# Delta-rule attention and an expert router on one core: chunks of 32 tokens of all four sequences in place of 64 tokens of two, and two expert tiles beside the last chunks

## The chip, the core and the metric

The kernel runs on one core of a Trainium2 chip. A core has TensorE (PE, matrix products; PEld are its weight loads), VectorE (DVE), ScalarE (ACT), GpSimd (POOL), and queues that start DMA transfers (SP is the engine whose queue starts most of them here). Each engine works through its own list of instructions in the order in which the program gives them; engines wait for each other by semaphores. Matrix products read SBUF and write PSUM, eight banks of 512 fp32 columns on 128 partitions. The metric is device microseconds (us) of one launch. The profile is one more execution, so its span differs a little from the times.

## The reference

Four sequences of 768 tokens, eight heads of 48 columns. Each head of each sequence has a state of 48x48, which every token changes (the delta rule). The outputs, with the heads side by side, are 3072 rows of 384, and go through a router to one of eight experts each.

```python
k_n = k / (np.linalg.norm(k, axis=-1, keepdims=True) + 1e-06)
for t in range(S):                                   # 768 tokens
    y[:, :, t] = einsum('bhd,bhde->bhe', q[:, :, t], state)
    v_old = einsum('bhde,bhd->bhe', state, kt)
    state = state + bt * einsum('bhd,bhe->bhde', kt, vt - v_old)
# x: (3072, 384)
logits = xn @ en.T / tau                             # rows and expert embeddings normed
expert_idx = argmax(logits, axis=1);  gate_w = softmax(logits)[expert_idx]
for e in range(8):
    h = np.maximum(x[mask] @ w1[e], 0.0)             # w1[e]: 384 x 1024
    out[mask] = gate_w[mask, None] * (h @ w2[e])     # w2[e]: 1024 x 384
```

All products are in fp32.

## The kernel before

The tokens are handled in chunks. Inside a chunk, the rule becomes products with a triangular matrix and its inverse, which is built by doubling blocks: from inverses of 2x2 blocks to 4, 8, 16 and 32. A *unit* is one chunk of 64 tokens of two sequences: 128 rows (partitions), 16 matrices of 64x64 (two sequences, eight heads). There are 12 chunks times two pairs of sequences, 24 units; the two pairs alternate, so a unit needs the state that the unit two before it left. All small products go through one helper line, `mm` (L286), which is why most groups of the profile have that line; the tile names tell them apart.

```python
C = 64
PERIOD = 20
HALF = (slice(0, C), slice(C, 2 * C))
def mm(out_, lhsT, rhs, start=True):
    nc.tensor.matmul(out_, lhsT=lhsT, rhs=rhs, start=start, stop=True, skip_group_check=True)
# ... cut: loads, norms of k (prep1..3; the power is GpSimd's), transposes of K and Q by TensorE
def flip(src):                       # 128x128 transposes by TensorE, two 64x64 blocks each
    p = bank(jc)
    for j in range(NP):
        nc.tensor.transpose(p[:, j]..., src[:, j]..., ident)
    return p
def t_flip(U, eng):
    p = flip(U["W"])
    U["T"] = work("T", 3)
    eng(U["T"], p)
def product(lhsT, rhs):              # input half a, output half b: all four 64x64 tiles
    p = pair([NP, C])
    for j in range(NP):
        for a in range(2):
            for b in range(2):
                mm(p[HALF[b], a, j], lhsT[HALF[a], j, b], rhs[HALF[a], j, b])
    return p.rearrange("p a j c -> p j a c")
def level(U, s, by):
    p = product(U["A"][by], U["T"])
    U["P"] = PP[s][U["n"] % 2]
    nc.vector.copy_predicated(U["P"], below[s].broadcast_to(jc), p)
def grow(U):
    p = product(U["P"], U["W"])
    U["W"] = work("W", 5)
    act_copy(U["W"], p)
def apply(lhsT, rhs):                # input half = output half
    p = bank([128, H, D])
    for h in range(H):
        for i in range(2):
            mm(p[HALF[i], h], lhsT[HALF[i], h // 2, h % 2], rhs[HALF[i], h])
    return p
def solve1(U): ...  # Z1 = first half of apply(W, R)
def solve2(U): ...  # R += second half of apply(A, Z1)
def solve3(U): ...  # Z = apply(W, R): the step from 32 to 64 tokens
# ... cut: gram (16 products of 128 columns), q_state and k_state (16 each), state (16), outputs (apply),
#          x_transposes, logits (two halves), route1..3: choice of the expert, ranks, gate
def route4(c, xc, ssx, lz):          # once for two chunks
    for g in range(G):               # G = 4: running counts of each expert
        nc.vector.tensor_tensor(rk[:, 0, g], rk[:, 0, g], run, op=ALU.add)
        nc.vector.tensor_tensor(run, run, rk[:, 1, g], op=ALU.add)
    # ... cut: slot_i, each token's place in its expert's list
    for g in range(G):
        nc.gpsimd.indirect_dma_start(out=idmap[:, :],
            out_offset=bass.IndirectOffsetOnAxis(ap=slot_i[:, g:g + 1], axis=0),
            in_=K["tokid"][:, c - 1 + g // NU, g % NU:g % NU + 1], in_offset=None)
PLAN = [(-60, load_kq), (-46, prep1), (-42, prep2), (-36, prep3), ..., (5, gram), (9, a_flip),
        (13, lambda U: level(U, 2, 1)), (16, grow), (19, lambda U: t_flip(U, nc.vector.tensor_copy)), ...]
steps = [(U["n"] * PERIOD + at, i, U["n"]) for U in UNITS for i, (at, _) in enumerate(PLAN) if i or U["n"]]
for _, i, n in sorted(steps): ...    # this order is the order of each engine's list
```

Then come the experts. A tile is 128 rows of one expert. Eight lists of unknown length need at most 24 + 7 = 31 tiles, and 31 are always run; each fetches its list of rows, its expert's weights (two transfers of 1536 KB) and its rows.

```python
NT = N // T + E - 1                  # 31
ahead = [fetch(0), fetch(1)]
xT = transposed(ahead[0][-1])
for i in range(NT):
    now = ahead.pop(0)
    if i + 2 < NT:
        ahead.append(fetch(i + 2))
    nxT = transposed(ahead[0][-1]) if ahead else None
    experts(xT, *now)                # 24 products of 128 columns, Relu, 8 products of 384 columns
    xT = nxT
```

Of the kernel before, what the change touches and what calls it, by code (L numbers as in the profile page):

```python
# [13 lines left out]
SP = mybir.EngineType.SP  # L14

C = 64
T = 128
LEVELS = (2, 4, 8, 16)


@with_exitstack
def kernel(
# [35 lines left out]


# [3 lines left out]
    NU = B // 2  # L63
# [3 lines left out]
    NMAP = E * N + NT * T  # L67
# [4 lines left out]
    run = cpool.tile([128, E], F32, name="run")  # L72
    K = {}
    x_dram = tc.dram_tile([N + 1, Dm + 1], F32, name="x_dram")
    idmap = tc.dram_tile([NMAP, 1], I32, name="idmap")

    def bank(shape):
        return ps.tile(shape, F32, name="bank", tag="bank", bufs=2)

    def pair(shape):  # L80

        t = ps.tile([128, 2, 512], F32, name="pair", tag="pair", bufs=3)
        n = 1
        for d in shape:
            n *= d
        t = t[:, :, 0:n]
        if len(shape) == 2:
            return t.rearrange("p r (a b) -> p r a b", a=shape[0])
        return t.rearrange("p r (a b c) -> p r a b c", a=shape[0], b=shape[1])
# [7 lines left out]
    hc = [128, H, C]  # L97
    jc = [128, NP, 2, C]


    def padded(name, bufs):

        ts = []
        for i in range(bufs):
            t = ac.tile(hc, F32, name=f"{name}{i}")
            nc.gpsimd.memset(t[:, :, D:C], 0.0)
            ts.append(t)
        return ts

    def load(U, dst, src):  # L110

        t0 = U["c"] * C
        for i in range(2):
            nc.sync.dma_start(out=dst[i * C:(i + 1) * C],
                              in_=src[2 * U["u"] + i, :, t0:t0 + C, :].rearrange("h p d -> p h d"))

    def load_kq(U):
        U["k"] = io.tile([128, H, D], F32, name="k_in", tag="k_in", bufs=4)
        load(U, U["k"], k)
        U["Q"] = QQ[U["n"] % len(QQ)]  # L120
        load(U, U["Q"][:, :, 0:D], q)
# [5 lines left out]
    UNITS = [dict(n=n, c=n // NU, u=n % NU) for n in range(NC * NU)]  # L127
    QQ = padded("QQ", 4)
    load_kq(UNITS[0])
    bt = ac.tile([NU * H, NC, 2, C], F32, name="bt")  # L130
    for u in range(NU):
        for i in range(2):
            nc.scalar.dma_start(out=bt[u * H:(u + 1) * H, :, i],
                                in_=beta[2 * u + i].rearrange("h (c t) -> h c t", t=C))
    emb = ac.tile([E, Dm], F32, name="emb")
    nc.scalar.dma_start(out=emb, in_=moe_expert_emb)
    rtau = ac.tile([128, 1], F32, name="rtau")
    nc.scalar.dma_start(out=rtau, in_=moe_tau.broadcast_to([128, 1]))
# [4 lines left out]
    half = cpool.tile([128, NU, H], F32, name="half")  # L143
    nc.vector.memset(half, 0.5)
    KK = padded("KK", 6)


    prow = ac.tile([128, C], I32, name="prow")
    nc.gpsimd.iota(prow, pattern=[[0, C]], base=0, channel_multiplier=1)
    xor_i = ac.tile([128, C], I32, name="xor_i")  # L150
    nc.gpsimd.iota(xor_i, pattern=[[1, C]], base=0, channel_multiplier=0)
    trow = ac.tile([128, C], I32, name="trow")
    nc.vector.tensor_single_scalar(trow, prow, C - 1, op=ALU.bitwise_and)
    col_f = ac.tile([128, C], F32, name="col_f")
    nc.vector.tensor_copy(col_f, xor_i)
    nc.vector.tensor_tensor(xor_i, xor_i, trow, op=ALU.bitwise_xor)
    xor_f = ac.tile([128, C], F32, name="xor_f")
    nc.vector.tensor_copy(xor_f, xor_i)
    trow_f = ac.tile([128, C], F32, name="trow_f")
# [3 lines left out]
    id64 = ac.tile([128, 1, C], F32, name="id64")  # L163
    nc.vector.tensor_single_scalar(id64[:, 0, :], xor_f, 0.0, op=ALU.is_equal)
    upper = ac.tile([128, 1, C], F32, name="upper")
    nc.vector.tensor_tensor(upper[:, 0, :], col_f, trow_f, op=ALU.is_gt)
    lower = ac.tile([128, 1, C], F32, name="lower")
    nc.vector.tensor_tensor(lower[:, 0, :], col_f, trow_f, op=ALU.is_lt)

    def filled(name, bufs, value):  # L170

        ts = []
        for i in range(bufs):
            t = ac.tile(jc, F32, name=f"{name}{i}")
            nc.scalar.activation(t.rearrange("p j r c -> p (j r) c"), id64.broadcast_to(hc), ACT.Copy, scale=value)
            ts.append(t)
        return ts

    def mask(name, tri, lo, hi):
        m = ac.tile([128, 1, 1, C], F32, name=name)  # L180
        nc.vector.scalar_tensor_tensor(out=m[:, 0], in0=xor_f.unsqueeze(1), scalar=float(lo), in1=tri,
                                       op0=ALU.is_ge, op1=ALU.mult)
        nc.vector.scalar_tensor_tensor(out=m[:, 0], in0=xor_f.unsqueeze(1), scalar=float(hi), in1=m[:, 0],
# [3 lines left out]
    W2 = filled("W2_", 2, -1.0)  # L187
    T2 = filled("T2_", 2, -1.0)
    up2 = mask("up2", upper, 1, 2)
    below = {s: mask(f"below{s}", lower, s, 2 * s) for s in (1,) + LEVELS}  # L190


    psB = bank([128, NC, NU * H])
    for c in range(NC):
        nc.tensor.transpose(psB[:, c], bt[:, c].rearrange("p i t -> p (i t)"), ident[0:NU * H, 0:NU * H])
    betaT = ac.tile([128, NC, NU * H], F32, name="betaT")
    nc.vector.tensor_copy(betaT, psB)
    sqb = ac.tile([128, NC, NU * H], F32, name="sqb")
    nc.scalar.activation(sqb, betaT, ACT.Sqrt)
    quot = ac.tile([128, NC, NU * H], F32, name="quot")  # L200
    nc.vector.tensor_scalar_max(sqb, sqb, 1e-30)
    nc.vector.reciprocal(quot, sqb)
# [487 lines left out]
```

## Time and profile before

| what | value |
|---|---|
| median of 2 runs | 902.03 us (900.04 to 904.02) |
| span of the profile | 888.4 us, mean TensorE clock 0.919 |
| busy PE / DVE / ACT / POOL | 738.4 / 292.1 / 245.9 / 224.1 us |
| last copy of logits (end of attention but for the routing) | 497.9 us |
| first matmul of an expert's hidden layer | 541.7 us |
| last result of an expert (y) | 878.6 us |

The costliest groups of the page:

```profile
L639 PE MATMUL acc<-xTm,w 128*128 128x128 f32 x1488 | 172.3, 276 | 0.0
L644 PE MATMUL acc<-w,hT 128*128 128x384 f32 x496 | 165.1, 486 | 0.0
L286 PE MATMUL pair<-W,P 64*64 64x64 f32 x3072 | 75.9, 232 | 42.1 <-DVE P L376 35.0
L286 PE MATMUL bank<-Z,G 64*64 64x48 f32 x1536 | 60.4, 231 | 5.2 <-issue 4.1
L286 PE MATMUL bank<-R,W 64*64 64x48 f32 x1536 | 59.5, 230 | 0.9 <-issue 0.6
L346 PE MATMUL bank<-ident,W 128*128 128x128 f32 x288 | 49.2, 295 | 11.1 <-ACT KT L362 10.1
```

A line names the engine, the operation, the output tile, an arrow and the inputs, then the shape and the number of instructions; after the bar stand busy time in us and the mean ns of one, after the second bar the idle time before it and who ended it. An fp32 product is two instructions: 24 units x 4 steps x 16 products of `grow` are 1536, and the row with W and P has 3072. Matmuls are pipelined, so the mean of one (232 ns) is not the distance between two.

### The profile page before, as it was taken

Reading aid. Unit: us, or ns where it says so; the run is one execution under the profiler, and the core shown is the slowest. Engines: PE = TensorE matmul, PEld = TensorE weight load, DVE = VectorE, ACT = ScalarE, POOL = GpSimd, SP = SyncE. Lnnn points to the kernel's source line nnn. Section 1 sums busy time; section 2 is a strip of 40 time slices with the busy share of each in tenths; the row PEclk is TensorE's granted clock in tenths of the full one; section 3 lists DMA queues with packets and bytes.
Section 4 is the critical chain, followed back from the end, with each engine's and each line's share of the span. In section 5 each row is a group of like instructions: output and inputs, shape, how many; then the busy total and the mean of one; then the engine's idle time right before and its main releaser. Section 6 shows DMA issues by size and latency. Waiting matters only on the chain. (4 is left out here: it accounts for less than half of the span.)

```text
span 888.4 us, 33205 instructions
## 1 busy us (share of the span) xinstructions
PE 738.4 (83%) x15148; PEld 632.6 (71%) x15148; DVE 292.1 (33%) x692; ACT 245.9 (28%) x468; POOL 224.1 (25%) x240
## 2 busy tenths in 40 slices
PE   1589998598599859897988306999999999999995
PEld 1578887587588758787877205888888877777774
DVE  5356555356265625544553400000000000000000
ACT  4245453254344324533433100111111111111110
POOL 4543341333243233414111111121111111111110
PEclk9799997799989769978989657999999999999998
DMA  4332122122221211120010149999999999999940
GB/s 85 77 66 49 31 53 52 20 52 40 45 49 35 62 29 35 27 48 3 5 39 4 36 152 374 322 321 326 329 321 329 314 341 327 320 315 320 318 163 1
DMA packets 134190, 129.64 MB, mean 146 GB/s; under 512 B 84538, under 2 KB 119521, under 8 KB 134050
## 3 DMA queue, kind: packets, MB, share of 16 engines
q1 hardware_dynamic: 128738, 116.55, 43.0%
q0 software_dynamic: 4736, 10.85, 3.6%
q8 instruction: 119, 1.95, 0.9%
q10 hardware_dynamic: 576, 0.11, 0.1%
q14 instruction: 21, 0.17, 0.1%
HBM read 117.91 MB, written 10.95 MB: 145 GB/s over the span
## 5 line engine op out<-in xcount | busy, mean ns | idle before, releaser
L639 PE MATMUL acc<-xTm,w 128*128 128x128 f32 x1488 | 172.3, 276 | 0.0
L639 PEld LDWEIGHTS acc<-xTm,w 128*128 128x128 f32 x1488 | 169.9, 193 | 0.3
L644 PE MATMUL acc<-w,hT 128*128 128x384 f32 x496 | 165.1, 486 | 0.0
L644 PEld LDWEIGHTS acc<-w,hT 128*128 128x128 f32 x496 | 91.9, 190 | 57.5
L641 ACT ACTIVATE hT<-acc 128x512 f32<-128x512 f32 x62 | 37.0, 597 | 337.5 <-PE acc L639 291.3
L646 DVE TENSOR_SCALAR y<-acc,xg 128x384 f32<-128x384 f32 x31 | 19.1, 617 | 304.2 <-PE acc L644 304.2
L286 PE MATMUL pair<-W,P 64*64 64x64 f32 x3072 | 75.9, 232 | 42.1 <-DVE P L376 35.0
L286 PEld LDWEIGHTS pair<-W,P 64*64 64x64 f32 x3072 | 66.0, 144 | 45.0 <-DVE P L376 36.2
L362 ACT ACTIVATE W<-pair 128x512 f32<-128x512 f32 x96 | 57.5, 599 | 119.8 <-PE pair L286 118.6
L376 DVE COPY_PREDICATED P<-below,pair 128x512 f32<-128x512 int32 x96 | 70.5, 735 | 49.4 <-PE pair L286 49.4
L647 POOL DMA_INDIRECT out_dram<-y,ids x31 | 31.5, 1016 | 164.1 <-DVE y L646 161.4
L301 POOL TENSOR_TENSOR rn<-rn,half 128x8 f32<-128x8 f32 x24 | 39.5, 1646 | 110.4 <-DVE rn L300 109.6
L286 PE MATMUL bank<-Z,G 64*64 64x48 f32 x1536 | 60.4, 231 | 5.2 <-issue 4.1
L620 POOL DMA_INDIRECT xg<-x_dram,ids x31 | 30.0, 968 | 136.1 <-DMA ids<-idmap 73.7
L286 PE MATMUL bank<-R,W 64*64 64x48 f32 x1536 | 59.5, 230 | 0.9 <-issue 0.6
L286 PEld LDWEIGHTS bank<-Z,G 64*64 64x64 f32 x1536 | 55.4, 147 | 6.8 <-issue 4.7
L346 PE MATMUL bank<-ident,W 128*128 128x128 f32 x288 | 49.2, 295 | 11.1 <-ACT KT L362 10.1
L538 POOL DMA_INDIRECT idmap<-tokid,slot_i x24 | 23.8, 991 | 132.8 <-DMA idmap<-tokid,slot_i 65.6
L286 PEld LDWEIGHTS bank<-R,W 64*64 64x64 f32 x1536 | 55.8, 148 | 1.5 <-issue 0.6
L629 PE MATMUL acc<-ident,xg 128*128 128x128 f32 x93 | 16.0, 283 | 38.8 <-DMA xg<-x_dram,ids 38.8
L629 PEld LDWEIGHTS acc<-ident,xg 128*128 128x128 f32 x93 | 12.3, 146 | 48.5 <-issue 35.7
L286 PE MATMUL pair<-T,AJ 64*64 64x64 f32 x1536 | 43.3, 244 | 3.5 <-DVE T L354 2.8
(161 smaller groups left out, 895.5 us busy)
## 6 DMA issues: line engine op xcount, KB each, us to landing
w<-in_moe_w_dram SPq DMA_DIRECT2D x62, 1536.0 KB
x_dram<-xc SPq DMA_DIRECT2D x24, 192.5 KB
k_in<-in_k_dram SPq DMA_DIRECT2D x48, 96.0 KB
QQ<-in_q_dram SPq DMA_DIRECT2D x48, 96.0 KB
v_in<-in_v_dram SPq DMA_DIRECT2D x48, 96.0 KB
ids<-idmap SPq DMA_DIRECT2D x31, 0.5 KB
xg<-x_dram,ids POOLq DMA_INDIRECT x31, 6.6
out_dram<-y,ids POOLq DMA_INDIRECT x31, 7.1
```

What stands on the lines that cost most here:

```text
L286: nc.tensor.matmul(out_, lhsT=lhsT, rhs=rhs, start=start, stop=True, skip_group_check=True)
L301: nc.gpsimd.tensor_tensor(out=U["rn"], in0=U["rn"], in1=half[:, 0], op=ALU.pow)
L346: nc.tensor.transpose(p[:, j].rearrange("p r c -> p (r c)"), src[:, j].rearrange("p r c -> p (r c)"), ident)
L362: nc.scalar.activation(out_, in_, ACT.Copy)
L376: nc.vector.copy_predicated(U["P"], below[s].broadcast_to(jc), p)
L538: nc.gpsimd.indirect_dma_start(out=idmap[:, :], out_offset=bass.IndirectOffsetOnAxis(ap=slot_i[:, g:g + 1], axis=0), in_=K["tokid"][:, c - ...
L620: nc.gpsimd.indirect_dma_start(out=x, out_offset=None, in_=x_dram[:, :], in_offset=bass.IndirectOffsetOnAxis(ap=ids[:, 0:1], axis=0))
L629: nc.tensor.transpose(psX[:, j, :], x[:, j * 128:(j + 1) * 128], ident)
L639: nc.tensor.matmul(psH[:, i, :], lhsT=w1[:, j, (f + i) * 128:(f + i + 1) * 128], rhs=xT[:, j, :], start=(j == 0), stop=(j == KC - 1))
L641: nc.scalar.activation(hT[:, f:f + 4, :], psH, ACT.Relu)
L644: nc.tensor.matmul(psO, lhsT=hT[:, f, :], rhs=w2[:, f, :], start=(f == 0), stop=(f == NF - 1))
L647: nc.gpsimd.indirect_dma_start(out=out[:, :], out_offset=bass.IndirectOffsetOnAxis(ap=ids[:, 0:1], axis=0), in_=y, in_offset=None, bounds_ ...
```

## The change

A unit becomes one chunk of 32 tokens of all four sequences: again 128 rows and 24 units, but 32 matrices of 32x32, two of which share a 64x64 block. Now each unit needs the state that the unit just before it left. The doubling ends at 32 tokens, so one solve step is enough. Transposes inside the doubling are made by VectorE in 32x32 blocks, in place of TensorE's 128x128. The fixed period is replaced by a table of places (KEYS and BASE) that orders all parts, and a part can be split in stages. PSUM banks are handed out by hand. List entries of one group are declared free of one another; the last group is smaller (two units). Early tiles: after 16 chunks the first two tiles of expert 0's list are taken, and worked on beside the last units, with expert 0's weights loaded during attention. The rest of the experts' tiles run under two branches, so that tiles beyond the count are skipped in steps.

```diff
-C = 64
+C = 32
+PC = 2 * C
+GROUP = 4
+AHEAD_AT = 16
+AHEAD = 2
...
+    CORNERS = ((0, 0), (1, 1), (0, 1), (1, 0))
...
+    def transposed_blocks(U, src):
+        U["T"] = wk.tile([128, H, C], F32, name="T", tag=f"T{U['n'] % 3}", bufs=1)
+        nc.vector.transpose(U["T"].rearrange("p h c -> p (h c)"), src.rearrange("p h c -> p (h c)"))
...
+    def apply(lhsT, rhs, at=by_number, rat=by_number, to=None, times=1):
+        n = rhs.shape[2]
+        p = bank([128, times, H, n])
+        for h in range(H):
+            for i in range(2):
+                (half_, l), (_, r) = at(i, h), rat(i, h)
+                own = HALF[half_]
+                mm(p[own, :, (to or rat)(i, h)[1]], lhsT(i, h) if callable(lhsT) else lhsT[own, l],
+                   rhs[own, r].unsqueeze(1).broadcast_to([PC, times, n]))
+        return p if times > 1 else p[:, 0]
+    def crossed(lhsT, rhs, at, rat):
+        p = pair([2, NP, C])
...
+                    mm(p[HALF[half_ ^ jj], half_, :, j], lhsT[own, l], rhs[own, r].unsqueeze(1).broadcast_to([PC, 2, C]))
...
+    def level(U, s):
+        p = apply(G, U["T"], at, at, times=2)
+        yield
+        nc.vector.copy_predicated(U["P"]..., below[s]..., p...)
+    def grow(U, s):
+        p = crossed(U["P"], U["W"], PLACE[s], PLACE[s])
+        yield
+        nc.vector.transpose(U["T"]..., p...)
+        yield
+        act_copy(U["W"]..., p)
...
+    def of_states(U):            # K and Q against the state, 32 products; then
+        nc.vector.scalar_tensor_tensor(out=R, in0=ps_[1], scalar=K["second"], in1=V, ...)
+        nc.vector.scalar_tensor_tensor(out=R, in0=ps_[0], scalar=K["first"], in1=R, ...)
+    def solve(U):
+        p = apply(U["W"], U["R"], inside, by_parity, by_number)
+        yield
+        for b, name in enumerate(("first", "second")):
+            act_copy(U["Zx"][:, :, b], p, K[name])
+        yield
+        act_copy(U["Z"], p)
+    def state(U):                # 16 products of 96 columns, then one sum by VectorE
...
+    def put_on_lists(i):
+            if i > 0:
+                nc.gpsimd.memset(gap, 0.0)
+            put = nc.gpsimd.indirect_dma_start(out=idmap[:, :], ...)
+            # i == 0: after the entries of the group before; otherwise:
+                tc.declare_no_dep(put.ins, group=f"lists{g['n']}", reason="tokens' lists: distinct places")
...
+    STEPS["snap"], STEPS["next"] = last_unit(snap), lambda U: None
+    for i in range(AHEAD):
+        STEPS[f"early_x{i}"] = last_unit(early_x, i)
+        for f in range(0, NF, 2):
+            STEPS[f"early_h{i}_{f}"] = last_unit(early_hidden, i, f)
+        STEPS[f"early_o{i}"] = last_unit(early_result, i)
+    KEYS = {"load": (-7729, -7728), ..., "gram": (-3748, -3747, -3418, -3417), ...,
+        "early_o1": (20460, 20461, 20462, 20463, 23089, 23090), ...}
+    BASE = (-22140, -20199, -18130, ..., 22724)
...
+    work_through(0, parts[0], parts[1])          # parts = [22, 26, 31]
+    with tc.If(count > parts[0]):
+        work_through(parts[0], parts[1], parts[1])
+        with tc.If(count > parts[1]):
+            ...
```

## The prediction

> **What bounds the kernel now.** I read the page's slices first, then busy times by stretch, then the waits of one stretch of the attention stage, and last TensorE's work in order of time, for the cost of one step.
>
> ```profile
> PE   1589998598599859897988306999999999999995
> PEclk9799997799989769978989657999999999999998
> ...
> 70.00:109.00 39.00, 36.55 (x1368) 33.70 (x1361) 22.27 (x43) 19.36 (x38) 10.85 (x11) 1.00 0.20 38
> 147.00:186.00 39.00, 27.90 (x918) 25.41 (x920) 15.57 (x32) 14.15 (x28) 14.73 (x14) 0.87 0.19 33
> 500.00:520.00 20.00, 1.03 (x4) 0.93 (x4) 6.71 (x37) 0.00 (x0) 3.92 (x4) 0.50 0.15 40
> 520.00:540.00 20.00, 0.87 (x3) 0.50 (x3) 0.56 (x1) 0.00 (x0) 1.94 (x2) 0.50 0.79 299
> 700.00:800.00 100.00, 100.00 (x613) 79.55 (x612) 9.74 (x18) 11.35 (x19) 17.85 (x18) 1.00 0.97 323
> ```
>
> A row of the stretches gives length, busy PE, PEld, DVE, ACT, POOL, then clock, DMA share, GB/s. Three stages show. To 498 us: attention, TensorE busy 94% in a good stretch (70 to 109) and 72% in a bad one. From 498 to 541 us: TensorE nearly idle, clock halved. From 541 us: experts, TensorE full at full clock. There, 31 tiles end between 541.5 and 878.6 us, 10.87 us each; one tile's matmuls at the end take 5.36 us (hidden) and 5.16 (result), so TensorE sets this pace, DMA (0.97) just behind.
>
> The logits' copies mark the units of attention: 79.32, 95.67, 111.61, 126.93 us, so 15.9 us a unit; over the steady stage it is more (state updates at 70.9 and 474.1 us, 21 units apart: 19.2 us). The difference comes once for each routing group (two chunks of two units). The waits of the bad stretch, 147 to 186 us:
>
> ```profile
> POOL idmap L538 <- DVE slot_i L536: 14.0, 1, 14.0
> DVE rn L306 <- POOL rn L301: 13.5, 1, 13.5
> POOL idmap L538 <- DMA idmap<-tokid,slot_i: 12.1, 3, 4.4
> PEld pair L286 <- DVE P L376: 10.0, 1, 10.0
> PE pair L286 <- DVE P L376: 9.9, 1, 9.9
> ```
>
> Read from the third line: four scatters of list entries each wait for the one before to land, 4 us. GpSimd stands still meanwhile, the norm's power waits behind them in its queue, VectorE waits for that power, and what VectorE owes TensorE comes 10 us late. 19.2 - 15.9 = 3.3 us a unit, 13 a group, fits.
>
> The cost of each step at full clock is the distance between starts in TensorE's order, 440 to 475 us:
>
> ```profile
> 441.79 1.02 PE L286 MATMUL bank<-Z,G 64*64 64x48 f32 x29
> 442.60 0.27 PE L286 MATMUL pair<-W,P 64*64 64x64 f32 x1
> ...
> 446.32 0.66 PE L346 MATMUL bank<-ident,W 128*128 128x128 f32 x4
> 446.90 0.52 PE L286 MATMUL bank<-enT,xT 128*64 128x8 f32 x12
> ...
> 449.60 0.66 PE L286 MATMUL pair<-W,P 64*64 64x64 f32 x30
> 450.08 0.22 PE L286 MATMUL pair<-T,G 64*64 64x64 f32 x1
> ...
> 473.35 0.68 PE L286 MATMUL pair<-Z,KK 64*64 64x48 f32 x32
> 473.85 0.66 PE L286 MATMUL pair<-W,P 64*64 64x64 f32 x32
> ```
>
> A step of 16 fp32 products is 32 instructions. `product` (all four tiles, 64 columns): 0.48/30 = 16 ns each, 0.51 us. `apply` (only the two diagonal tiles, 48 columns): 0.81/29 = 28 ns, 0.89 us. Four flips: 0.58 us. State: 0.50. By the same reading gram is 0.87 and the two state reads 1.08.
>
> **What the Trainium skill says.** "TensorEngine Tiling (Array Packing)", Tiling Modes, Key Properties: tiles execute weight loads and matmuls in parallel. The trace agrees: four tiles at 16 ns with 64 columns, two at 28 with fewer. Its section Performance Considerations, PSUM Bottleneck, warns that eviction may then bind; before the change ACT and DVE are half busy, so not yet. "TensorE: Matmul & The Clock Gate", Part 1, says that idling halves the clock; the trace shows 0.50 in the gap, and the same 29 `apply` instructions over 1.83 us at 457.50 instead of 1.02. "VectorE: DVE Perf Modes", The three transpose paths: VectorE transposes only 32x32 blocks. No run here shows its cost yet.
>
> **The change part by part.**
>
> *TensorE per unit.* Both kernels have 24 units of 128 rows. Before: 8 `product` 4.1, 4 `apply` 3.6, 4 groups of flips 2.3, gram 0.87, state reads 1.08, state 0.50, 8 transposes 1.16, x transposes 0.42, logits 0.45: 14.4 us. Against the period of 15.9, a factor 1.10. After: flips are gone (VectorE transposes), two of three solve steps are gone (four levels complete a 32-token inverse), logits are halved to 0.22. The four `grow` steps keep four tiles (`crossed`): 2.05. But the four `level` steps now go through `apply`, whose row and output halves are the same: two tiles, 64 columns. I scale 28 ns by 64/48 to 37, 1.19 us a step: 4.75, against 2.05 before. So a part of the gain is given back, whatever the name of the change. Solve and outputs 1.78; state with 96 columns, between 0.50 at 48 and gram's 0.87 at 128: 0.72; gram, state reads, transposes and x transposes as before, 3.53; routing about 0.2. Sum 13.25. Times 1.10: 14.6 us a unit.
>
> *The other engines.* From rows of the page, an ACT eviction is 597 ns for 512 columns, 491 for 384, so about 390 for 256, and 90 more with a scale from a tile. Fifteen evictions of 256 to 512 columns plus Zx, Yq, Z, xT and the square sum to 11.0 us. DVE: four predicated copies 2.94, two of half size 0.93, four block transposes 1.8 (estimate: a copy's rate), two residual passes 1.23, state with 768 columns 0.95, xc 0.56, norm 1.0, routing and logits 0.9: 10.3. Both remain below 14.6. GpSimd gets 6.3 us of arithmetic and one scatter a unit.
>
> *The stall in each group.* The scatters of one group are declared free of one another and spread by the table between other parts. I take the 3.3 us a unit away wholly.
>
> *The new recurrence.* A unit now needs the state of the unit just before it, where two interleaved chains gave slack. At these durations: state reads 1.1, two DVE passes 1.3, solve 0.9, two ACT evictions 1.2, state 0.7, DVE sum 0.95, and some 0.2 us for each of five handovers: 7.2 us. That fits twice into 14.6.
>
> *Attention's sum.* First logits come 60.6 us after the first transposes (18.7 us). Three flips with their copies (1.5 us each) and two solve steps with theirs (1.9 each) leave the chain, a pass of 0.6 on each level enters: I take 7 off, 72 us. Then 23 x 14.6 = 336. The last units run faster (gaps 14.5, 9.0 and 5.6 us before, 19 less than three periods); the first early tile fills that drain with about 9. Last logits: 72 + 336 - 19 + 9 = 398 us, against 498.
>
> *Experts.* From the reference's inputs the router gives the experts 385, 377, 351, 388, 365, 351, 421 and 434 tokens, and 276 tokens of expert 0 in the first 16 chunks. So both early tiles are full (256 tokens), 129 remain, and the tiles after are 2+3+3+4+3+3+4+4 = 26. The second bound in the code is also 26, so 26 run in place of 31, and the five for leftover are skipped: 26 x 10.87 = 282.6 instead of 337.
>
> *The gap.* Before: 43.6 us from the last logits to the first matmul of an expert, with 17 us in four scatters, and the first weights asked for at 522 and used at 541. After: expert 0's weights are there and scatters don't wait in line. Left over: routing 4.5 us, the second early tile (10.9 us of TensorE, which fills most of it), and then the first gather: it stands in GpSimd's queue behind the last early result, and takes about 3.5 us, plus 1.5 for transposes and copy. About 23 us with small delays. Weights of tile 1 can be asked for only after the tile table (5 us of DVE), so they arrive about as tile 0 ends.
>
> *Sum.* 398 + 23 = 421; + 282.6; + 3 for two branches (a guess, nothing in this trace has one); + 10 from the last result to the end (878.6 to 888.4 before): 716 us of profile. The median is 902.03 where the profile has 888.4, a factor 1.015: 727 us.
>
> **Rivals.** *TensorE's period does not fall*: the two-tile levels cost more than scaled, or the in-order queues stall on the longer ACT and DVE lists. For it: 11 and 10 us of 14.6 are near enough that any late eviction holds the next step. Against: undisturbed the kernel runs within 10% of its TensorE sum already. At 16 us a unit: 759 us measured; at the old 19.2, 834. *ACT and DVE become the bound only in bursts and the searched order packs TensorE fully*: 13.3 us a unit, 697. *The recurrence binds*: if each handover took 1 us, the loop would be 11 us, still under the period; it would need a queue order that puts other parts in between. *DMA bound in the experts*: 0.97 busy before; tile 0 needs no load, so I expect no loss, but if tile 1's weights are late by a tile, 10 us more.
>
> **Range and chances.** The unit's period is the widest term: 1.5 us either way is 35 us. Gap and branches add 10. I take 695 to 770. Even with no gain in attention, five tiles (54 us) and half of the gap leave over 8%. Faster by over 2%: 0.97; within 2%: 0.02; slower: 0.01.
>
> **What would show it.** Logits' copies 14.6 us apart, first near 72, last near 398. Level steps of 32 instructions near 1.2 us, twice a grow step. No wait of GpSimd on its own scatters that reaches TensorE. 26 x 48 hidden-layer instructions in the expert stage, at 10.9 us a tile. A gap near 23 us filled by the early tile. I would be wrong if the level steps took two times their scaled cost, if waits on VectorE or ScalarE stood ahead of TensorE in each unit, or if the branch stopped the engines for many microseconds.

## The result, and the profile after

The changed kernel takes 703.42 us (median of 2 runs, 702.27 to 704.57), where the kernel before takes 902.03: a ratio of 0.780, with an interval of 0.771 to 0.789. The prediction was 727 us, with a range of 695 to 770.

The slices of the page of the changed kernel, to be held against the first two lines shown of before. Each digit is a slice of 17.5 us in tenths:

```profile
PE   3788999989988988999999999999999999999992
...
PEclk9999999999999999999999999999999999999997
```

The pits in TensorE's row during attention, and the deep one (3, 0) between attention and experts, are gone, and the granted clock is at 0.9 or more in every slice but the last.

The stretches (length, busy PE, PEld, DVE, ACT, POOL, then clock, DMA share, GB/s); the first two are steady attention, the third is the gap, the last the experts:

```profile
83.00:169.00 86.00, 79.22 (x2802) 74.39 (x2801) 59.24 (x130) 55.38 (x134) 43.05 (x45) 1.00 0.36 75
169.00:256.00 87.00, 80.55 (x2807) 75.71 (x2809) 59.58 (x141) 53.77 (x133) 46.23 (x50) 1.00 0.32 71
...
385.00:400.00 15.00, 15.00 (x83) 11.18 (x82) 7.39 (x42) 1.75 (x5) 5.27 (x6) 1.00 0.18 59
500.00:600.00 100.00, 100.00 (x612) 79.96 (x611) 10.58 (x18) 10.75 (x18) 17.89 (x18) 1.00 0.94 328
```

In steady attention TensorE is busy 92 to 93% of the time, VectorE 69% and ScalarE 62 to 64%: TensorE's list still sets the pace, with the other two nearer than before. The logits' copies, which mark the units, come at 70.34 us first, 83.19 second, 342.63 twentieth and 384.64 last: (342.63 - 83.19)/18 = 14.41 us a unit in the steady stage.

The waits of the steady stage, 83 to 343 us, first TensorE's, then two of GpSimd's on its scatters (total, times, longest):

```profile
PE psum L377 <- issue: 10.0, 19, 1.5
PE psum_pair L377 <- issue: 8.8, 14, 1.9
```

```profile
POOL idmap L728 <- issue: 1.9, 11, 0.2
POOL idmap L728 <- DVE slot_i L696: 1.3, 4, 0.3
```

In before's bad stretch, GpSimd stood 14.0 us for its scatter's index and 12.1 for scatters in flight, and TensorE 9.9 for VectorE. Now neither is there. What TensorE still waits for is "issue", about 1 us a unit: time in which it waited for nothing that the profile shows.

TensorE's order of work, for the cost of a step (start, duration, operation, count; a step's cost is the distance between starts):

```profile
213.78 0.28 PE L377 MATMUL psum<-T,G 64*64 64x64 f32 x4
...
214.71 1.03 PE L377 MATMUL psum<-Z,M 64*64 64x48 f32 x30
...
215.63 0.64 PE L377 MATMUL psum_pair<-W,P 64*64 64x64 f32 x29
216.06 0.21 PE L377 MATMUL psum_pair<-state,KT 48*64 48x48 f32 x1
```

A level step of 32 instructions, 64 columns on two tiles, takes 214.71 - 213.78 = 0.93 us, 29 ns each. Outputs with 48 columns, which begin at 214.71, take 28. A grow step on four tiles still runs at 0.43/29 = 15 ns.

The gap between the last logits and the first hidden layer:

```profile
384.64 0.17 DVE L633 COPY lz<-psum 128x8 f32<-128x8 f32 x1 [2.53 <-PE psum L377]
...
390.83 5.52 PE L782 MATMUL psum<-space,w_first 128*128 128x128 f32 x48
...
396.19 5.33 PE L793 MATMUL psum<-w_first,space 128*128 128x384 f32 x16
...
402.32 0.52 PE L937 MATMUL acc<-ident,xg 128*128 128x128 f32 x3 [0.81 <-issue]
...
403.64 5.62 PE L946 MATMUL acc<-xTm,w_first 128*128 128x128 f32 x48 [0.80 <-DVE xTm L938]
```

It is 19.0 us, and the second early tile (the 48 instructions of its hidden layer at 390.83, the 16 of its result up to 401.5) fills it. TensorE waits there only twice, for 0.8 us, the clock granted from 385 to 400 is 1.00, and the hidden layer at 403.64 takes 5.62 us.

Two tiles further on, in the same view:

```profile
590.22 5.52 PE L946 MATMUL acc<-xTm,w 128*128 128x128 f32 x48
...
601.07 5.52 PE L946 MATMUL acc<-xTm,w_first 128*128 128x128 f32 x48
```

A tile takes 10.85 us. The last result comes at 687.7 us, 284.1 after the first hidden product: 26 tiles.

Where 187.8 us of profile (888.4 - 700.6) went, by stage:

| stage | before | after | difference |
|---|---|---|---|
| start to the last logits | 497.9 | 384.6 | -113.3 |
| last logits to the first hidden product | 43.8 | 19.0 | -24.8 |
| expert tiles | 336.9 | 284.1 | -52.8 |
| last result to the end | 9.8 | 12.9 | +3.1 |

The profile of before is of an execution that took 890.14 us, 12 less than the median, so by the medians 198.6 us are gained, and the table leaves some 11 of them without a place.

The experts and the gap went as argued. The questions are in attention: what is worth what there?

### The profile page after: what moved, and what is told of

Its sections match the earlier page's. It is cut to its first block, busy times and chain, and to the rows that moved or that the text cites. A ratio compares the mean times of both kernels' runs of the same rounds, so it can differ in the third digit from the quotient of the medians.

```text
span 700.6 us, 29275 instructions
## 1 busy us (share of the span) xinstructions
PE 638.8 (91%) x13031; PEld 557.2 (80%) x13031; DVE 290.0 (41%) x698; ACT 260.8 (37%) x611; POOL 243.6 (35%) x277
## 5 line engine op out<-in xcount | busy, mean ns | idle before, releaser
L377 PE MATMUL psum<-T,G 64*64 64x64 f32 x2304 | 107.9, 222 | 10.4 <-issue 8.0
L377 PEld LDWEIGHTS psum<-T,G 64*64 64x64 f32 x2304 | 94.2, 138 | 12.1 <-issue 9.1
L946 PEld LDWEIGHTS acc<-xTm,w 128*128 128x128 f32 x816 | 93.8, 192 | 4.5
L946 PE MATMUL acc<-xTm,w 128*128 128x128 f32 x816 | 93.9, 275 | 0.0
L953 PE MATMUL acc<-w,hT 128*128 128x384 f32 x272 | 90.5, 486 | 0.0
L526 DVE COPY_PREDICATED P<-below,psum 128x512 f32<-128x512 int32 x96 | 70.2, 731 | 38.2 <-PE psum L377 27.9
L377 PE MATMUL psum_pair<-W,P 64*64 64x64 f32 x3072 | 75.0, 226 | 9.7 <-issue 5.2
L377 PEld LDWEIGHTS psum_pair<-W,P 64*64 64x64 f32 x3072 | 61.6, 136 | 15.6 <-issue 9.4
L955 DVE TENSOR_SCALAR y<-acc,xg 128x384 f32<-128x384 f32 x26 | 16.1, 618 | 125.0 <-PE acc L953 125.0
L377 PE MATMUL psum<-T,Gx 64*64 64x64 f32 x768 | 51.2, 224 | 3.3 <-issue 3.3
L946 PE MATMUL acc<-xTm,w_first 128*128 128x128 f32 x432 | 49.8, 275 | 0.8 <-DVE xTm L938 0.8
```

The source lines that it names most:

```text
L526: nc.vector.copy_predicated(U["P"].rearrange("p h (b c) -> p h b c", b=2), below[s].rearrange("p o (b c) -> p o b c", b=2).broadcast_to([1 ...
L946: nc.tensor.matmul(psH[:, i, :], lhsT=t.w1[:, j, (f + i) * 128:(f + i + 1) * 128], rhs=t.xT[:, j, :], start=(j == 0), stop=(j == KC - 1))
L953: nc.tensor.matmul(psO, lhsT=t.hT[:, f, :], rhs=t.w2[:, f, :], start=(f == 0), stop=(f == NF - 1))
L955: nc.vector.tensor_scalar_mul(y, psO, t.x[:, Dm:Dm + 1])
```

## The experiments

Each run is compared with the kernel before, run on the same chip beside it (medians of 903 to 907 us); the ratios are to that. Each trace is of one execution. For the kernels with 8-byte rows and with levels 32 columns wide, one execution over 1.5% above the shortest is left out of the median. Where an interval overlaps that of the changed kernel (0.771 to 0.789), the difference between the two is given, but is within what the measurement leaves open.

### The scatters: waiting, spreading, and the width of a row

The prediction takes 3.3 us a unit off because scatters no longer wait for each other. But the change does three things to them: it declares them free, places them apart by its table, and (a line that the prediction passed over) writes 64 bytes for each token in place of 4: `ROW, ID = Dm + 16, 16`, where a list's row has ID words. The theory of the prediction is that the wait for the scatter before costs the 3.3 us and the declaration removes it. The rivals: the table's places alone hide the wait, and the narrow rows are the harm. Five kernels separate these.

**The kernel before, its four scatters declared free.**

```diff
         for g in range(G):
-            nc.gpsimd.indirect_dma_start(out=idmap[:, :], ...)
+            if g > 0:
+                nc.gpsimd.memset(gap, 0.0)
+            put = nc.gpsimd.indirect_dma_start(out=idmap[:, :], ...)
+            # g == 0: after the group before; otherwise:
+                tc.declare_no_dep(put.ins, group=f"lists{c}", reason="distinct places")
```

> The kernel before, with one edit: the four scatters of list entries of a group no longer wait for one another (a group still waits for the group before, and the lists' readers wait for the last group). Theory of the prediction: the wait costs 3.3 us a unit, 13 us a group, so the state updates come 15.9 us apart in place of 19.2, attention ends about 75 us earlier, and the last four scatters in the gap take 5 us in place of 17, 12 us more: about 815 us. Rival: the wait only hides another one (norms, loads), and TensorE's waits move: then less than 30 us are gained, about 875 us or more.

Measured: 916.24 us, ratio 1.012 (1.007 to 1.017). The gain did not come; the kernel is slower. The timeline behind one group of scatters, in order of time:

```profile
246.51 0.13 PEld L287 LDWEIGHTS pair<-W,P 64*64 64x64 f32 x1 [0.28 <-issue]
253.66 1.22 PE L287 MATMUL pair<-W,P 64*64 64x64 f32 x21 [7.28 <-issue]
...
254.19 1.09 ACT L335 ACTIVATE G<-pair 128x512 f32<-128x512 f32 x2 [9.38 <-remote]
```

and the stretches around it:

```profile
243.00:248.00 5.00, 3.38 (x67) 3.36 (x66) 0.92 (x4) 0.49 (x1) 0.83 (x1) 0.68 0.38 25
248.00:252.00 4.00, 0.00 (x0) 0.00 (x0) 0.00 (x0) 0.00 (x0) 0.00 (x0) 0.70 0.65 39
```

TensorE stops in the middle of a grow step, after 11 of its 32 instructions, for 7.28 us, and the profile names nothing that it waits for. Behind the three other groups of this trace it stops in the same way, for 3.5, 2.0 and 6.4 us. From 248 to 252 no engine does any work, while the DMA engines are busy 65% of the time and move only 39 GB/s. So the wait for the scatter before was removed, and something worse came in its place.

**The same with rows of 64 bytes.**

```diff
-    idmap = tc.dram_tile([NMAP, 1], I32, name="idmap")
+    idmap = tc.dram_tile([NMAP, 16], I32, name="idmap")
-        c["tokid"] = ac.tile([128, NC, NU], I32, name="tokid")
+        c["tokid"] = ac.tile([128, NC, NU, 16], I32, name="tokid")
```

> The kernel before with scatters of a group free of one another, as in the run that came out slower, and the rows of the list 64 bytes wide in place of 4, as the changed kernel has them. Theory D (entries of 4 bytes are what holds up the other engines when four scatters are under way together): the stall of some 10 us a group goes, state updates come 16 us apart and attention ends some 75 us earlier: 815 to 835 us. Rival E (four scatters in a row hold up the others whatever their width): no better than with 4 bytes, 905 us or more.

Measured: 847.72 us, 0.934 (0.926 to 0.943). Against the run above, only the row's width differs: 68 us. The stall of all engines is gone; a scatter lands in 2.3 us. But the time is above the range expected: a unit takes 17.6 us, not 15.9, and routing groups still stick out. GpSimd still stands before its scatters, 75 to 440 us:

```profile
POOL idmap L543 <- DVE slot_i L539: 64.7, 5, 13.9
```

Once in each group it reaches them some 13 us before VectorE has their places, and stands there with the next norm's power behind it, as in before (14.0 in its bad stretch). But this no longer reaches TensorE. Its waits on VectorE's P, the last link of the prediction's chain, are, in before and in this run, 75 to 440 us:

```profile
PE pair L286 <- DVE P L376: 30.8, 4, 9.9
```

```profile
PE pair L287 <- DVE P L377: 2.2, 1, 2.2
```

What is left in each group is another wait, which the prediction overlooked. ScalarE's copy of KT stands behind the exponential of the routing, which waits for VectorE, and TensorE stands for that copy:

```profile
140.45 0.65 PE L347 MATMUL bank<-ident,W 128*128 128x128 f32 x4 [2.52 <-ACT KT L363]
...
143.14 1.83 PE L287 MATMUL bank<-Z,G 64*64 64x48 f32 x29
...
149.04 1.02 PE L287 MATMUL bank<-Z,G 64*64 64x48 f32 x30
```

```profile
110.00:130.00 20.00, 18.00 (x639) 16.33 (x638) 11.01 (x21) 9.90 (x19) 6.09 (x6) 1.00 0.17 34
130.00:150.00 20.00, 16.92 (x506) 15.62 (x509) 11.30 (x32) 8.53 (x16) 5.51 (x6) 0.83 0.32 73
150.00:170.00 20.00, 17.94 (x662) 16.23 (x655) 11.75 (x29) 9.79 (x19) 11.24 (x13) 1.00 0.19 35
```

Behind the wait the granted clock is down (0.51 from 143 to 149 us), and 29 instructions take 1.83 us, where 30 take 1.02 six us later. The copies of logits around it come at 116.17, 132.03, 154.83 and 170.97 us: 15.9, 22.8, 16.1. So one unit in four is 7 us longer, 1.7 us a unit, which is what 17.6 has over 15.9. TensorE has four such waits of 2.3 to 2.5 us here, and four of 2.5 us in before; the changed kernel has none from 83 to 343 us. That the short wait brings the clock down is not shown by a run of its own.

**The kernel before with rows of 64 bytes alone, its scatters one after another.**

```diff
-    idmap = tc.dram_tile([NMAP, 1], I32, name="idmap")
+    idmap = tc.dram_tile([NMAP, 16], I32, name="idmap")
```

> The kernel before with only the width of the list's rows changed to 64 bytes; each scatter still waits for the one before it. Theory D: a scatter lands in about 2.6 us as in the changed kernel, not 4.0, so GpSimd's stand in each group shrinks by 3 x 1.4 us and the last group too: 870 to 895 us. If the width alone removes the stall: 830 us. Rival E: same as before within 5 us, about 904 us.

Measured: 880.27 us, 0.971 (0.964 to 0.979); landing takes 2.5 us in place of 4.0, and from 75 to 440 us GpSimd waits 29.4 us for scatters under way, not 46.0. As expected of a wait that is made shorter and stays: wide rows alone give 3%. Its units take 18.9 us each, where before has 19.2.

**The changed kernel with its scatters one after another again.**

```diff
-            else:
-                tc.declare_no_dep(put.ins, group=f"lists{g['n']}", reason="tokens' lists: distinct places")
```

> The changed kernel, with each scatter waiting again for the one before it; the places of the scatters in the table stay. Theory A (the freed wait is what gains): four waits of 4 us a group in GpSimd's queue come back, and with them some 10 us a group, so 50 us or more: 750 us or above. Theory B (the table alone hides the wait, since it puts about 8, 9 and 4 us of other work between the scatters): under 8 us, mostly in the last group, where two scatters stand on the path to the first expert tile: 705 to 711 us.

Measured: 708.34 us, 0.782 (0.778 to 0.786), 5 us over the changed kernel by the medians and 2 by the ratios, with overlapping intervals. This is what the rival expected whose table hides the wait: once the scatters are spread and wide, it hardly matters whether they may overlap.

**The changed kernel with rows of 8 bytes.**

```diff
-    ROW, ID = Dm + 16, 16
+    ROW, ID = Dm + 16, 2
```

> The changed kernel with the list's rows 8 bytes wide in place of 64 (row of x and row of the output, nothing else is stored); scatters stay free of one another and spread by the table. Theory D (narrow entries hold up the other engines): about what the kernel before lost with four free narrow scatters against four free wide ones, some 10 us a group of four, so 40 to 60 us more: 740 us or above. Rival B (with scatters spread over a period, a narrow one does no harm): within 8 us of the changed kernel, below 712 us.

Measured: 720.10 us, 0.795 (0.791 to 0.799), 17 us over the changed kernel by the medians and 13 by the ratios. TensorE's "issue" waits, 75 to 440 us, are 30.4 us against 21.9 in the changed kernel, and the mean granted clock from 83 to 343 us is 0.93 against 1.00. This is between the two expectations: narrow rows harm even where scatters are spread, but less than where four come in a row. What was not run is wide, free scatters bunched in the changed kernel, or the table's spacing in the kernel before.

Side by side, medians in us (902 to 907 for the kernel before):

| | one after another | free |
|---|---|---|
| before, 4-byte rows | 902 | 916 |
| before, 64-byte rows | 880 | 848 |
| changed, 64-byte rows, spread by the table | 708 | 703 |
| changed, 8-byte rows, spread | not run | 720 |

### What a level step on two tiles costs

The prediction scales 28 ns at 48 columns to 37 at 64. The changed kernel shows 29, so the rival is a fixed time for each instruction on two tiles. And if two tiles cost twice what four do, four should be the better form.

**The changed kernel with its level products 32 columns wide.** Each level product makes two equal copies side by side; here one is made, and VectorE reads it twice. What is computed stays the same.

```diff
-        p = apply(G, U["T"], at, at, times=2)
+        p = apply(G, U["T"], at, at, times=1)
```

> The changed kernel, with the level products 32 columns wide in place of 64 (the second copy of the columns is read twice by VectorE from the same place; the result is the same). In the changed kernel 48 columns on two tiles take 27.5 ns an instruction and 64 take 29. Theory A (as in the prediction, time in proportion to columns): 15 ns, a level step 0.5 us, 1.7 us a unit less of TensorE's work and some 30 to 40 us less: 665 to 675 us. Theory B (the load of 64 weight columns and the stream follow each other on the same tile, each with a part of the time): about 21 ns, 0.25 us a step, 15 to 25 us less. Theory C (a fixed time for each instruction on two tiles): 27 ns, no gain beyond 5 us.

Measured: 724.12 us, 0.804 (0.799 to 0.808): slower by 21 us, with half of the columns. TensorE's order of work in this kernel:

```profile
204.49 0.25 PE L377 MATMUL psum<-T,G 64*64 64x32 f32 x4
...
205.39 1.06 PE L377 MATMUL psum<-Z,M 64*64 64x48 f32 x30
```

0.90 us for 32 instructions, 28 ns each: with 32, 48 or 64 columns, a product on these two tiles takes the same time. That settles the rate in favour of the fixed time. The loss, which no theory expected, goes with a lower clock in the stretches:

```profile
83.00:169.00 86.00, 80.32 (x2752) 76.34 (x2751) 57.87 (x126) 55.02 (x133) 42.47 (x44) 0.96 0.36 73
...
256.00:343.00 87.00, 80.06 (x2592) 75.85 (x2592) 55.43 (x126) 52.35 (x128) 44.13 (x49) 0.92 0.27 60
```

TensorE is as busy as in the changed kernel, but the clock granted is 0.92 to 0.96 in place of 1.00. It is so in every execution: over the whole kernel the mean clock is 0.946 to 0.963, where the changed kernel has 0.981 and 0.987. This trace is of the shortest one, 715.42 us; its last logits come 13 us later than the changed kernel's. Why narrower products go with a lower clock isn't shown.

**The changed kernel with its levels on all four tiles.** The products of odd heads go to the other half of the partitions and are not brought back, and VectorE copies the two banks apart. So routing and experts work on other values than the reference's; only attention's times are read.

```diff
-        p = apply(G, U["T"], at, at, times=2)
+        p = pair([2, NP, C])
+        ...     mm(p[HALF[half_ ^ jj], half_, :, j], G(i, h), U["T"][own, r]...)
```

> The changed kernel with the level products on all four tiles, as grow has them, and VectorE's copy in two halves; the results of odd heads land in the other half, so the output and the counts of the experts are not the reference's, and only the attention stage is read. Theory P (TensorE's list sets the period, and two tiles cost 0.93 us a step against 0.51): 1.7 us a unit less, first to last logits in about 275 us in place of 314, less what VectorE's 0.6 us more a unit takes. Rival Q (the level steps now need the two double banks of PSUM as well, and wait for them): no gain or a loss, 310 us or more, with TensorE waiting for VectorE's or ScalarE's copies out of those banks.

Measured: 793.52 us, 0.878 (0.874 to 0.882). Attention, which alone is to be read, takes 403.2 us from the first to the last copy of logits, where the changed kernel takes 314.3 and theory P expected 275; a unit takes 18.8 us in place of 14.41. A step begins like this:

```profile
251.61 0.69 PE L377 MATMUL psum_pair<-T,G 64*64 64x64 f32 x32
253.80 0.69 PE L377 MATMUL psum_pair<-W,P 64*64 64x64 f32 x32 [1.50 <-DVE P L534]
255.76 0.54 PE L377 MATMUL psum_pair<-T,G 64*64 64x64 f32 x14 [1.27 <-ACT WL L428]
```

and TensorE's waits from 70 to 400 us are

```profile
PE psum_pair L377 <- DVE P L534: 25.0, 20, 1.6
PE psum_pair L377 <- ACT W L428: 17.8, 22, 1.5
PE psum_pair L377 <- ACT WL L428: 17.2, 16, 1.6
```

The step does run faster (its last instruction ends after 0.69 us), but it writes two banks, as grow does, and now TensorE stands for the copy that frees a pair: the products T,G of the third line don't read WL, so what they wait for is the pair. These waits are 60 us in the 330, about three in a unit, 3.4 us of it. The clock granted from 83 to 343 us is 0.82. Rival Q came true. With this table and two pairs of banks, the two tiles in a single bank are thus the better choice, though their products cost twice as much; a table searched for four tiles, or a third pair, was not run.

### Which engine sets the period

Three kernels add nearly the same work per unit to one engine each, by giving instructions twice, which leaves what is computed as it is. If TensorE's list sets the period, only the first should cost its full size; if the latency of the loop through VectorE and ScalarE does, the other two should cost as much.

**TensorE: the grow products twice** (2.05 us a unit).

```diff
+                    for _ in range(2):
                         mm(p[HALF[half_ ^ jj], half_, :, j], lhsT[own, l], rhs[own, r]...)
```

> The changed kernel with each of the four grow products issued twice (the second overwrites the first with the same values): 4 x 0.51 = 2.05 us more of TensorE's work in each unit, and as much more latency in a unit's chain. Theory P (TensorE's list sets the period): 24 x 2.05 = 49 us more, 745 to 755 us. Rival L (the latency of the chain or the handovers set it): about the same in all three runs of this kind, 20 us or more each. Rival S (slack on all engines): under 15 us.

**VectorE: the predicated copies of three levels twice** (2.2 us a unit).

```diff
+        for _ in range(1 if s == 16 else 2):
             nc.vector.copy_predicated(U["P"]..., below[s]..., p...)
```

> The changed kernel with the predicated copies of levels 2, 4 and 8 made twice (the second writes the same values): 3 x 0.73 = 2.2 us more of VectorE's work in each unit, and as much latency in the chain. Theory P: VectorE is busy 69% of the steady stage, so most of it fits: under 20 us more, below 724 us. Rival V (VectorE is as near the bound as TensorE): 40 us more or above, 743 us. Rival L (latency): as much as with TensorE's work doubled.

**ScalarE: the grow copies twice** (2.1 us a unit).

```diff
+        for _ in range(2):
             act_copy(U["W"]..., p)
```

> The changed kernel with ScalarE's copies of the grow steps made twice (the second writes the same values): 3 x 0.38 + 2 x 0.47 = 2.1 us more of ScalarE's work in each unit, and as much latency in the chain. Theory P: ScalarE is busy 64% of the steady stage: under 20 us more, below 724 us. Rival L (latency): as much as with TensorE's work doubled.

Measured:

| doubled on | median us | ratio (interval) | over the changed kernel | per unit (24) |
|---|---|---|---|---|
| TensorE | 790.51 | 0.872 (0.863 to 0.882) | +87.1 | 3.6 |
| VectorE | 713.97 | 0.788 (0.779 to 0.797) | +10.6 | 0.44 |
| ScalarE | 710.03 | 0.784 (0.773 to 0.794) | +6.6 | 0.28 |

Added work of VectorE and ScalarE is hidden to four fifths or more; TensorE's is paid in full and more. (VectorE's and ScalarE's intervals overlap the changed kernel's, TensorE's is far from it. By the ratios the three differences are 84, 7 and 3 us.) So TensorE's list sets the period, and VectorE's and ScalarE's latency does not. The TensorE row is a surprise, though: 2.05 us were added, 49 us in sum, and 87 paid. In its timeline a doubled grow step of 64 instructions stops on the way:

```profile
250.63 0.91 PE L377 MATMUL psum_pair<-W,P 64*64 64x64 f32 x39
251.88 0.56 PE L377 MATMUL psum_pair<-W,P 64*64 64x64 f32 x19 [0.34 <-issue]
```

and the waits from 76 to 474 us are mostly of that kind:

```profile
PE psum_pair L377 <- issue: 31.9, 48, 2.1
PE psum L377 <- issue: 10.8, 16, 1.5
```

42.7 us in 23 units: 1.86 us a unit, where the changed kernel has about 1.0. The added 3072 instructions cost 87.1 us, 28 ns each, though within a burst they run at 16 to 18. Over 83 to 343 us the changed kernel completes 8442 TensorE instructions and this one 8457, both 32.5 a microsecond. A limit on how fast instructions reach TensorE, of about 31 ns each on the mean, would fit; but nothing here separates it from other causes, and the stretch of before from 70 to 109 us has 1368/39 = 35 a microsecond. It stays open.

No run gives the kernel before the shorter list of TensorE alone. That of the 4.8 us a unit between 19.2 and 14.41 some 1.5 are the shorter list (undisturbed units of before take 15.9) and the rest is the stall in each group, is read from the traces.

### The table's rhythm and the early tiles

**Starts of units at even distances** (1951 keys apart) in place of the table's uneven ones.

```diff
+    BASE = tuple(-22140 + 1951 * n for n in range(NC))
```

> The changed kernel with the units' starts in the table evenly spaced (1951 apart) in place of the searched ones (1902 to 2084 apart), everything else as it is. Theory P: the fine order matters little while TensorE's work is the same: within 5 us, 700 to 709 us. Rival O (the searched order is what lets TensorE run without waits): 10 us more or above, over 713 us, with waits on VectorE ahead of TensorE in some units.

Measured: 706.77 us, 0.780 (0.772 to 0.788), the changed kernel's ratio, though 3 us over its median. The gain is not in these fine shifts.

**No early tiles**, all 28 after attention.

```diff
-AHEAD = 2
+AHEAD = 0
```

> The changed kernel without early tiles: expert 0's first weights are still loaded during attention, no rows are taken ahead, and 28 tiles run after attention, as the token counts give. Theory A (the early tiles fill TensorE's idle time in the drain and in the gap): two tiles more, 21.7 us, less what the drain gets shorter (about 5 us) and what the gap gets shorter without the queue of early results (about 4 us): 12 us more, 715 us. Rival B: their work fits wholly into idle time, and nothing gets shorter without them: 22 us more, 725 us. Rival C: they only displace other work, and the time stays: 703 us.

Measured: 721.89 us, 0.800 (0.796 to 0.804), 18.5 us over the changed kernel, between theory A's 715 and rival B's 725; two tiles are 2 x 10.85 = 21.7 us, so the two early tiles cost about 3 us where they stand, nearly nothing. The last logits come at 384.0, where they come at 384.6 with an early tile in front of them; from the twentieth copy to the last it is 38.9 us without and 42.0 with it. The gap without early tiles, and the first hidden layer behind it:

```profile
384.00:400.00 16.00, 2.82 (x11) 2.24 (x11) 7.77 (x43) 0.21 (x1) 4.14 (x5) 0.50 0.19 54
```

```profile
400.02 7.90 PE L947 MATMUL acc<-xTm,w_first 128*128 128x128 f32 x48 [0.71 <-DVE xTm L939]
```

The gap is 16.0 us, only 3 shorter, with TensorE busy for 2.8 of them and its clock at 0.50, and the first 48 instructions behind it take 7.90 us in place of 5.62. With the second early tile in the gap the clock stays at 1.00.

## Why the prediction was right, point by point

The time lies in the range, 23.6 us below its centre, and the reasons carried: TensorE's sum sets the period, 26 tiles in place of 31, an early tile in the gap. One step of the mechanism failed: that the scatters' waiting for one another is the stall in each group, and that the declaration takes it away. Its number came out about right in sum, by other parts of the change. Three terms were mis-sized.

- *The period, 14.6 us.* Measured 14.41 in the steady stage. Three of its terms were off and nearly cancel. The level step, scaled with columns to 37 ns and 1.19 us, takes 29 ns and 0.93: 1.0 us a unit less. The scaling was the error: columns don't enter at 32 to 64. The Trainium skill, "TensorEngine Tiling (Array Packing)", Performance Considerations, Instruction Overhead, says that a product with one column takes as long as one with 60, and the run with 32 columns agrees (28 ns against 29); the prediction did not use it. Logits "halved to 0.22" take 0.69, since six instructions with 128x128 weights and 8 columns cost 0.115 us each: 0.47 more. The sum of steps is then 12.7 and the factor over it 1.14, not 1.10; about 1 us of the 1.7 between them is "issue".
- *Two tiles against four.* That levels on two tiles would cost twice a grow step is right (0.93 against 0.51). That this gave away part of the gain is not borne out: with four tiles and pairs of banks, and all else as it is, a unit takes 18.8 us. The same page, Gotcha 1 of its Restrictions and Gotchas, says that different row tiles cannot access one PSUM bank at the same time. The figures would fit it: the levels write one bank from both row halves, grow gives each half its own. Two tiles in two banks were not run, so whether the tiles or the bank set 29 ns stays open.
- *The stall in each group, 3.3 us a unit, taken away by declaring the scatters free.* This step failed. Declared free in the kernel before, they made it slower (1.012). Declared free with rows of 64 bytes they take away TensorE's wait on VectorE (30.8 to 2.2 us) and about half of the stall (19.2 to 17.6 us a unit): the chain that the prediction read was there, but it was not the whole, and the width of the rows, which it passed over, decides whether freeing them helps (68 us between the two runs). The other half, 1.7 us a unit, is TensorE's 2.5 us for ScalarE's KT behind the routing, and the low clock after it; the 13 us that GpSimd stands for its places cost little by then. The changed kernel has neither wait: its parts stand elsewhere in the lists, and the declaration itself is worth 5 us of 199 at most. How much of the low clock is a consequence of the waits is not shown: from 75 to 440 us it is 0.90 in before, 0.95 in before with free, wide scatters, 1.00 after.
- *Other engines below the bound.* Right: VectorE 69%, ScalarE 64%, and doubled copies are nearly hidden. The block transposes, estimated at 1.8 us for four, take 446 ns each from PSUM. The rival of packed TensorE at 13.3 us a unit, and the one of a binding ScalarE or VectorE, are out.
- *The recurrence fits.* Right as far as seen: no wait of TensorE from 83 to 343 us ends on VectorE or ScalarE.
- *Attention's sum, 398 us.* Measured 384.6. First logits 70.3 (predicted 72); 23 periods of 14.41 in place of 14.6 give 4 less; start and drain were 17 us shorter than 23 periods, where the prediction had 19 shorter less 9 for an early tile. An early tile costs the drain 3 us (42.0 against 38.9), not 9.
- *The gap, 23 us.* Measured 19.0, filled as described.
- *Experts, 282.6 + 3 for branches.* Measured 284.1 for 26 tiles with the branches in them; TensorE is busy 282.2 us of them, so no branch costs what can be seen. DMA, at 1.00 from 420 to 500 us and 0.94 from 500 to 600, did not bind.
- *The end, 10 us.* Measured 12.9; what added 3 wasn't looked for.
- *The factor from profile to median, 1.015.* Measured 703.42/700.6 = 1.004: 8 us of the 23.6. It was no such factor: the profiled execution of before took 890.14 us for a span of 888.4, that of the changed kernel 702.27 for 700.6, 1.7 us more each. The prediction took the distance between two executions of before for a cost of every launch. Attention's 13 and the gap's 4 make up the rest, less the end's 3 and the like.

## What to carry to other kernels

Before one counts a wait as gain, one asks what the engine behind it will do with the freedom: the same four scatters were a cost of 4 us each in line, a stall of all engines when let loose with 4-byte rows, and nothing that can be seen when wide and spread by the table. And one lists all waits of the engine that sets the period: here a wait of 2.5 us, once in a group, with a halved clock after it, was half of the stall. For small fp32 products count instructions, not columns: on two tiles in one bank each took 28 to 29 ns at 32, 48 and 64 columns, and the form on four tiles, which needs two banks, cost more in waits for copies than it saved. To find the engine that sets a period, double its work and the others' in turn: here 3.6 us against 0.44 and 0.28 a unit.

## What the runs showed of the hardware that was not expected

- Scatters of 128 rows of 4 bytes, four in a row and free of each other: TensorE stops for 2.0 to 7.3 us in each of four groups, in the worst of them all engines for 4 us, with DMA 65% busy at 39 GB/s; with rows of 64 bytes the same program is 68 us faster. How narrow rows stop TensorE in the middle of a step isn't known.
- After one wait of 2.52 us TensorE ran at a granted clock of 0.51 from 143 to 149 us; the unit took 7 us more than its neighbours.
- With level products of half the width the granted clock was lower (0.92 to 0.96 in place of 1.00) with TensorE as busy as in the changed kernel, and the kernel lost 21 us.
- TensorE pauses that end on nothing visible were longer with more instructions: 1.0 us a unit in the changed kernel, 1.86 with the grow products doubled, whose extra instructions cost 28 ns each in place of 16 to 18.
- The first 48 instructions of a hidden layer, after 16 us of a nearly idle TensorE, took 7.90 us in place of 5.62.
